# Seven tokens per row, earlier loads, and reciprocals on the GpSimd queue in an attention and maxout kernel

## The chip, the cores and the metric

The kernel runs on one core of one Trainium2 chip. The metric is the device time of one execution in microseconds (us). Before the change it was 395.11 us, the median of three runs (394.66 to 395.37).

The engines are called as in the profile: PE is TensorE, PEld its weight loads, ACT ScalarE, DVE VectorE, POOL GpSimd. SPq and POOLq are the DMA instructions that SyncE and GpSimd issue. Each engine works through its own list of instructions, and whatever stands at the head of the list holds what is behind it.

## The reference, cut to what matters

Softcapped attention feeds a maxout layer:

```python
# q, k, v: (8, 12, 448, 64) float32; w1, w2: (768, 1024); w_out: (1024, 768)
scores = 30 * tanh(scale * (q @ k.T) / 30)
attn = exp(scores - max) / sum(...)
x = (attn @ v) with heads side by side       # (3584, 768)
out = maximum(x @ w1, x @ w2) @ w_out         # (3584, 768) float32
```

## The kernel before

The 96 heads are worked in 48 pairs; one turn of the main loop, a "slot", is one pair. Three pairs form a group that is loaded and normalized together. The maximum is rewritten as x@w2 + relu(x@(w1-w2)), so the kernel first makes wd = w1-w2 and wm = w2@w_out (this is the "turn", "premultiply" and "subtract" below).

Three parts matter here. The first is how q and k arrive. A head has 448 rows, which is 3 x 128 + 64: partition p takes three neighbouring rows, and the last 64 rows come by transfers of their own. For the first four groups (12 pairs) TensorE turns them, and for the others a DMA transpose does:

```python
m, l = raw[g, what]                       # 3 x 128 rows, and the last 64
nc.sync.dma_start(out=m[...], in_=src[b, h0:h1, 0:NJ*P, :].rearrange("h (p j) d -> p h (j d)", j=NJ))
...                                       # [cut: one or two more for l]
for j in range(8):                        # transposes(i)
    nc.tensor.transpose(ps[:, j*P:(j+1)*P], kqf[g % 2][:, n, j, :], ident)
```

The second is the softmax sum. A row of sums leaves U, becomes 48 partitions, is inverted on VectorE, goes to DRAM and comes back broadcast to 64 partitions. All of these transfers are on the Sync queue. Then GpSimd multiplies:

```python
def invert(g, n0=0, n1=G):
    nc.vector.reciprocal(t[:m, :], sums[g, n0][:m, :])
    nc.sync.dma_start(out=d[:m, :], in_=t[:m, :])                  # rec_d <- rec_s
    for h in range(2):
        nc.sync.dma_start(out=rb[64*h:64*h+64, ...], in_=...to_broadcast(...))   # rec_b <- rec_d
def normalize(...):
    eng.tensor_mul(xT[b // 2][r, hp, cs], U[g][r, h, n, :], rec[g, n0][r, n - n0, :])
```

The third is the store of 128 finished rows. The row order of the output follows the row order of q:

```python
rows = out[b0*S : b0*S + NJ*P, :].rearrange("(p j) n -> p j n", j=NJ)
nc.sync.dma_start(out=rows[:, j, :], in_=osb)                      # 128 rows of 768
```

## Time and profile before

| | before |
|---|---|
| time, median of 3 runs | 395.11 us |
| span of the profiled run | 390.3 us |
| PE busy, PE idle | 358.5, 31.8 us |
| granted TensorE clock, mean | 0.983 |
| POOL busy | 199.6 us |

The busy lines and slices are shown in the prediction.

The waits of the kernel before: engine, line and tile that waited; what ended the wait; us in total, times, longest.

```profile
POOL xT L305 <- DMA rec_b<-rec_d: 73.8, 31, 8.3
DVE u L265 <- POOL xT L305: 24.7, 8, 4.5
```

GpSimd stands 73.8 us for broadcast reciprocals and this costs little, for TensorE waits for xT only 1.7 us. For the reciprocals GpSimd stands in this kernel only ahead of the multiplications that need the data.

### The profile page before, as it was taken

Reading aid. Unit: us, or ns where it says so; the run is one execution under the profiler, and the core shown is the slowest. Engines: PE = TensorE matmul, PEld = TensorE weight load, DVE = VectorE, ACT = ScalarE, POOL = GpSimd, SP = SyncE. Lnnn points to the kernel's source line nnn. Section 1 sums busy time; section 2 is a strip of 40 time slices with the busy share of each in tenths; the row PEclk is TensorE's granted clock in tenths of the full one; section 3 lists DMA queues with packets and bytes.
Section 4 is the critical chain, followed back from the end, with each engine's and each line's share of the span. In section 5 each row is a group of like instructions: output and inputs, shape, how many; then the busy total and the mean of one; then the engine's idle time right before and its main releaser. Section 6 shows DMA issues by size and latency. Waiting matters only on the chain.

```text
span 390.3 us, 5720 instructions
## 1 busy us (share of the span) xinstructions
PE 358.5 (92%) x2128; PEld 171.8 (44%) x2128; DVE 164.3 (42%) x248; ACT 292.4 (75%) x289; POOL 199.6 (51%) x254
## 2 busy tenths in 40 slices
PE   3468896999999999989998999999999999999995
PEld 1123443544444444434443445444444444455563
DVE  5332657774434533253325433352345333633421
ACT  2699995878899799978998899889998899400000
POOL 4272269674638374656657464729482733651000
PEclk9995998999999999999999999999999999999999
DMA  6998899786779768967989597969796751322022
GB/s 142 280 252 180 242 288 274 198 202 165 149 199 252 198 171 199 260 181 192 217 225 223 142 237 210 255 166 225 219 188 179 166 142 65 90 73 100 23 81 81
DMA packets 106596, 71.50 MB, mean 183 GB/s; under 512 B 61384, under 2 KB 99400, under 8 KB 106568
## 3 DMA queue, kind: packets, MB, share of 16 engines
q1 hardware_dynamic: 104616, 67.99, 67.6%
q0 software_dynamic: 1952, 3.15, 4.6%
q8 instruction: 16, 0.26, 0.3%
q14 instruction: 12, 0.10, 0.1%
HBM read 53.48 MB, written 11.18 MB: 166 GB/s over the span
## 4 chain that ended last, share of the span: by engine, by line
PE 54%; DMA 17%; ACT 7%; SPq 6%; POOL 6%; DVE 5%; issue 3%; POOLq 0%; DVEq 0%; ACTq 0%
PE mm L318 15%; PE mm L333 11%; PE mm L330 9%; PE pv L250 8%; DMA rec_d<-rec_s 7%; DMA rec_b<-rec_d 6%; POOL xT L305 6%; PE s L231 5%; ACT expo L238 3%; ACT tanh L232 3%; DMA vm<-in_v_dram 3%; PE pv L259 2%; SPq L112 2%; SPq L101 1%; DMA xT<-in_moe_w_dram 1%
## 5 line engine op out<-in xcount | busy, mean ns | idle before, releaser
L232 ACT ACTIVATE tanh<-s 128x896 bf16<-128x896 f32 x144 | 126.0, 909 | 36.2 <-PE s L231 35.9
L305 POOL TENSOR_TENSOR xT<-u,rec_b 64x448 bf16<-64x448 f32 x95 | 108.2, 1139 | 86.1 <-DMA rec_b<-rec_d 73.8
L238 ACT ACTIVATE expo<-tanh 128x1792 bf16<-128x1792 bf16 x96 | 144.9, 1510 | 3.0
L265 DVE COPY u<-pv 128x896 f32<-128x896 f32 x48 | 52.3, 1091 | 105.3 <-PE pv L259 80.6
L333 PE MATMUL mm<-wo_sb,gT 128*128 128x384 bf16 x448 | 88.8, 327 | 0.0
L318 PE MATMUL mm<-xT,wd_sb 128*128 128x448 bf16 x384 | 80.8, 353 | 3.3 <-POOL xT L305 1.7
L330 PE MATMUL mm<-wm_sb,xT 128*128 128x384 bf16 x336 | 68.0, 327 | 1.8 <-DVE osb L337 1.8
L250 PE MATMUL pv<-expo,vp 128*128 128x448 bf16 x288 | 66.3, 367 | 1.1 <-ACT expo L238 1.1
L333 PEld LDWEIGHTS <-gT 128*128 128x128 bf16 x448 | 41.9, 98 | 36.5 <-issue 10.8
L337 DVE COPY osb<-mm 128x384 f32<-128x384 f32 x56 | 31.0, 555 | 59.9 <-PE mm L333 54.9
L318 PEld LDWEIGHTS <-wd_sb 128*128 128x128 bf16 x384 | 35.4, 98 | 43.9 <-issue 14.5
L231 PE MATMUL s<-qkT 64*128 64x448 bf16 x288 | 46.0, 370 | 7.7 <-DVE qkT L210 5.2
L322 DVE TENSOR_SCALAR gT<-mm 128x448 bf16<-128x448 f32 x64 | 39.9, 623 | 29.6 <-PE mm L318 28.6
L330 PEld LDWEIGHTS <-xT 128*128 128x128 bf16 x336 | 31.7, 98 | 28.6 <-issue 8.7
L250 PEld LDWEIGHTS <-vp 128*128 128x128 bf16 x288 | 28.2, 101 | 29.1 <-issue 7.7
L132 POOL CAST kqf<-qm 128x1152 bf16<-128x1152 f32 x15 | 17.2, 1147 | 33.9 <-DMA qm<-in_q_dram 33.7
L235 ACT ACTIVATE tanh<-s 128x448 bf16<-128x448 f32 x48 | 26.0, 542 | 4.3 <-PE s L234 4.1
L124 POOL CAST vp<-vm 128x576 bf16<-128x576 f32 x30 | 19.9, 665 | 14.2 <-DMA vm<-in_v_dram 9.4
L132 POOL CAST kqf<-km 128x1152 bf16<-128x1152 f32 x15 | 17.2, 1147 | 12.7 <-DMA km<-in_k_dram 11.9
L231 PEld LDWEIGHTS <-qkT 64*128 64x128 bf16 x288 | 10.9, 96 | 22.8 <-issue 15.1
L209 PE MATMUL mm<-ident,kqf 128*128 128x128 bf16 x96 | 9.8, 248 | 11.5 <-DVE kqf L132 7.7
L186 PE MATMUL mm<-wo_sb,w2T 128*128 128x384 bf16 x96 | 18.7, 328 | 0.0
(44 smaller groups left out, 158.9 us busy)
## 6 DMA issues: line engine op xcount, KB each, us to landing
rec_b<-rec_d SPq DMA_DIRECT2D x30, 336.0 KB, 5.0
out_dram<-osb SPq DMA_DIRECT2D x24, 384.0 KB, 3.9
km<-in_k_dram SPq DMA_DIRECT2D x15, 576.0 KB, 7.0
qm<-in_q_dram SPq DMA_DIRECT2D x15, 576.0 KB, 4.5
vm<-in_v_dram SPq DMA_DIRECT2D x15, 576.0 KB, 4.4
xT<-in_moe_w_dram SPq DMA_DIRECT2D x6, 512.0 KB
wo_sb<-in_moe_w_out_dram POOLq DMA_DIRECT2D x4, 384.0 KB, 7.3
gT<-in_moe_w_dram POOLq DMA_DIRECT2D x6, 256.0 KB, 5.8
```

Of the source, the lines that this page charges most:

```text
L132: eng.tensor_copy(t[:, n0:n1, o : o + NJ, :].rearrange("p n j (h d) -> p n h j d", h=2), m[:, 2 * n0 : 2 * n1, :].rearrange("p (n h) (j d) ...
L231: nc.tensor.matmul(s[:, h, :S], t[r, j * P : (j + 1) * P], qTn[r, :])
L232: nc.scalar.activation(tanh[i][:, 2 * j : 2 * j + 2, :], s[:, :, :S], AF.Tanh, scale=scale / cap)
L238: nc.scalar.activation(expo[i][:, c0:c1, :], tanh[i][:, c0:c1, :], AF.Exp, scale=float(cap))
L250: nc.tensor.matmul(ps[:, h, :S], vp[g % 2][:, n, h, j, :], e[:, 2 * j + h, :], start=(j == 0), stop=False)
L265: nc.vector.tensor_copy(U[g][:, :, n, :], pvt[i][:, :, :S])
L305: eng.tensor_mul(xT[b // 2][r, hp, cs], U[g][r, h, n, :], rec[g, n0][r, n - n0, :])
L318: nc.tensor.matmul(ps[:, :S], wd_sb[:, c, f * P : (f + 1) * P], x[:, c, cs], start=(c == 0), stop=(c == KC - 1))
L322: nc.vector.tensor_relu(g[:, f, cs], ps[:, :S])
L330: nc.tensor.matmul(ps[:, : DM // 2], x[:, c, ts], wm_sb[:, c, hs], start=(c == 0), stop=False)
L333: nc.tensor.matmul(ps[:, : DM // 2], g[:, f, ts], wo_sb[:, f, hs], start=False, stop=(f == FC - 1))
L337: nc.vector.tensor_copy(osb[:, hs], ps[:, : DM // 2])
```

## The change

The intent is to take the start and one early hole away. In the first two batches, each partition takes seven neighbouring tokens (64 partitions a head, a run of 1,792 bytes), so k and q come in one transfer each. The price is 26 small transposes and one large one instead of eight, and another row order of the output. The reciprocals' transfers move from the Sync to the GpSimd queue, in two steps (invert, then spread), with casts placed around them. The w2 chunks still come one per slot, the first now ahead of the loop, and later groups are loaded earlier. In the loop, F(n) puts up to n matmuls of the weights' or the feed-forward part between the others.

```diff
+    def rows(t, b, h0, h1):
+        return t[b, h0:h1, :, :].rearrange("h (r j) d -> (h r) (j d)", j=R7)
...   [cut: loads and casts of k, q, v for the first four groups by these rows]
-        for j in range(8):
-            nc.tensor.transpose(ps[:, j * P : (j + 1) * P], kqf[g % 2][:, n, j, :], ident)
+        for c, to in todo:
+            for a in range(2):
+                r = slice(64 * a, 64 * a + 64)
+                nc.tensor.transpose(ps[r, to : to + 64], x[r, c : c + D], ident[r, r])
+        nc.tensor.transpose(ps[:, NJ * P : Q0], x[:, NJ * P : Q0], ident)
...
     def invert(g, n0=0, n1=G):
-        nc.sync.dma_start(out=d[:m, :], in_=t[:m, :])
+        nc.gpsimd.dma_start(out=d[:m, :], in_=t[:m, :])
+
+    def spread(g, n0=0, n1=G):
         for h in range(2):
-            nc.sync.dma_start(
+            nc.gpsimd.dma_start(
                 out=rb[64 * h : 64 * h + 64, : n1 - n0, :],
...
-                rows = out[b0 * S : b0 * S + NJ * P, :].rearrange("(p j) n -> p j n", j=NJ)
-                nc.sync.dma_start(out=rows[:, j, :], in_=osb)
+                if wide:
+                    ...   [cut: as before]
+                else:
+                    o = o.rearrange("(r j) n -> j r n", j=R7)
+                    nc.sync.dma_start(out=o[2 * j : 2 * j + 2, :, :], in_=osb)
...
-        e = 0 if g < NT else 2
+        e = 0 if g < NT else 2 if g < NT + 2 else 3
         at(3 * g - 6 - e, load, g, "k")
...   [cut: q, v and the casts follow; w2 chunk 1 + c in slot 1 + c; order of the start]
         F(4 if late else 8)
+        if i == N - 1:
+            invert(g, 0, G - 1)
+        elif i >= G and n == 0:
+            invert(g - 1)
...
         for f, a in todo[i]:
             f(*a)
+        if i == N - 1:
+            spread(g, 0, G - 1)
+        elif i >= G and n == 0:
+            spread(g - 1)
+        elif i >= G and n == 1:
+            normalize(g - 1)
...   [cut: the same calls taken away after the second F(6)]
```

More of the change, by code (lines that the diff above doesn't have):

```diff
@@ L40 @@
     NJ = 3
+    NT = 4
+    R7 = S // 64
     scale = 1.0 / (D ** 0.5)
@@ L69, with flat @@
     qf = [t[:, :, 4:8, :] for t in kqf]
+    def flat(g):
+        return kqf[g % 2].rearrange("p n j c -> p n (j c)")
     ident = const.tile([P, P], bf16, name="ident")
@@ L89, in half, with raw_of @@
         return slice(0, 64) if b % 2 == 0 else slice(64, P)
+    def rows(t, b, h0, h1):
+        return t[b, h0:h1, :, :].rearrange("h (r j) d -> (h r) (j d)", j=R7)
+    def raw_of(g, what):
+        if (g, what) not in raw:
+            raw[g, what] = stage.tile([P, 2 * L * NJ * D + (2 * L if what == "q" else L) * D], f32, name=what + "r")
+        t = raw[g, what]
+        m = t[:, : 2 * L * NJ * D].rearrange("p (h c) -> p h c", c=NJ * D)
+        l = t[:, 2 * L * NJ * D :].rearrange("p (h d) -> p h d", d=D)
+        return t, m, l
     def load(g, what, n0=0, n1=L):
@@ L94, in load @@
         src = {"k": k, "q": q, "v": v}[what]
-        if (g, what) not in raw:
-            raw[g, what] = (
-                stage.tile([P, 2 * L, NJ * D], f32, name=what + "m"),
-                stage.tile([P, 2 * L if what == "q" else L, D], f32, name=what + "l"),
+        t, m, l = raw_of(g, what)
+        if g < NT and what == "v":
+            x = rows(src, b, h0, h1).rearrange("(h r) c -> r h c", r=64)
+            for a in range(2):
+                nc.sync.dma_start(
+                    out=m[64 * a : 64 * a + 64, 2 * n0 : 2 * n1, :], in_=x[:, :, NJ * D * a : NJ * D * (a + 1)]
+                )
+            for par in range(2):
+                nc.sync.dma_start(
+                    out=l[64 * par : 64 * par + 64, n0:n1, :], in_=x[:, par::2, 2 * NJ * D :]
+                )
+            return
+        if g < NT:
+            nc.sync.dma_start(
+                out=t[:, n0 * S : n1 * S].rearrange("p (n c) -> p n c", c=S),
+                in_=rows(src, b, h0, h1).rearrange("(n p) c -> p n c", p=P),
             )
-        m, l = raw[g, what]
+            return
         nc.sync.dma_start(
@@ L119, in cast @@
         b = g * L // NP
-        m, l = raw[g, what]
+        x, m, l = raw_of(g, what)
         if what == "v":
@@ L128, in cast @@
                 eng.tensor_copy(vl[g % 2][r, n0:n1, r], l[r, n0:n1, :])
+            return
+        if g < NT:
+            x = x[:, n0 * S : n1 * S].rearrange("p (n c) -> p n c", c=S)
+            if what == "q":
+                eng.tensor_copy(flat(g)[:, n0:n1, Q0 : Q0 + S], x)
+                return
+            eng.tensor_copy(flat(g)[:, n0:n1, : NJ * P], x[:, :, : NJ * P])
+            for par in range(2):
+                r = slice(64 * par, 64 * par + 64)
+                eng.tensor_copy(kf[g % 2][r, n0:n1, 3, r], x[r, :, NJ * P :])
             return
@@ L207, in transposes @@
         ps = mm_psum.tile([P, 512], f32, name="mm").bitcast(bf16)
-        for j in range(8):
-            nc.tensor.transpose(ps[:, j * P : (j + 1) * P], kqf[g % 2][:, n, j, :], ident)
-        nc.vector.tensor_copy(qkT_of(g)[:, n, :, :].rearrange("p j c -> p (j c)"), ps)
+        x = flat(g)[:, n, :]
+        todo = [(j * D, (j % 3) * P + (j // 3) * 64) for j in range(6)]
+        odd = i // NP % 2
+        todo += [(Q0 + j * D, Q0 + (64 * j if not odd else 0 if j == 6 else 64 + 64 * j)) for j in range(R7)]
+        for c, to in todo:
+            for a in range(2):
+                r = slice(64 * a, 64 * a + 64)
+                nc.tensor.transpose(ps[r, to : to + 64], x[r, c : c + D], ident[r, r])
+        nc.tensor.transpose(ps[:, NJ * P : Q0], x[:, NJ * P : Q0], ident)
+        nc.vector.tensor_copy(qkT_of(g)[:, n, :, :].rearrange("p j c -> p (j c)")[:, : Q0 + S], ps[:, : Q0 + S])
     def cross(g):
@@ L221, in qk @@
         t = qkT[g][:, n, :, :].rearrange("p j c -> p (j c)")
-        o = Q0 + 64 * (i // NP % 2)
+        o = Q0 + (64 * (i // NP % 2) if g >= NT else 0)
         qTn = t[:, o : o + S]
@@ L278, in gather @@
             )
+    recd = {}
     def invert(g, n0=0, n1=G):
@@ L283, in invert @@
         nc.vector.reciprocal(t[:m, :], sums[g, n0][:m, :])
-        d = dram.tile([16 * G, 56], f32, name="rec_d")
-        nc.sync.dma_start(out=d[:m, :], in_=t[:m, :])
+        d = recd[g, n0] = dram.tile([16 * G, 56], f32, name="rec_d")
+        nc.gpsimd.dma_start(out=d[:m, :], in_=t[:m, :])
+    def spread(g, n0=0, n1=G):
         rb = rec[g, n0] = xpool.tile([P, G, S], f32, name="rec_b")
-        flat = d[:m, :].rearrange("(h n a) c -> h n (a c)", h=2, a=8)
+        lines = recd[g, n0][: 16 * (n1 - n0), :].rearrange("(h n a) c -> h n (a c)", h=2, a=8)
         for h in range(2):
-            nc.sync.dma_start(
+            nc.gpsimd.dma_start(
                 out=rb[64 * h : 64 * h + 64, : n1 - n0, :],
-                in_=flat[h : h + 1, :, :].to_broadcast([64, n1 - n0, S]),
+                in_=lines[h : h + 1, :, :].to_broadcast([64, n1 - n0, S]),
             )
@@ L337, in moe @@
                 nc.vector.tensor_copy(osb[:, hs], ps[:, : DM // 2])
+            wide = b * NP >= NT * L
             if t == 3:
                 for n in range(2):
-                    r0 = (b - 1 + n) * S + NJ * P
-                    nc.sync.dma_start(out=out[r0 : r0 + 64, :], in_=osb[64 * n : 64 * n + 64, :])
-            else:
-                b0, j = (b, t) if t < 3 else (b, t - 4)
-                rows = out[b0 * S : b0 * S + NJ * P, :].rearrange("(p j) n -> p j n", j=NJ)
-                nc.sync.dma_start(out=rows[:, j, :], in_=osb)
+                    o = out[(b - 1 + n) * S : (b + n) * S, :]
+                    to = o[NJ * P : S, :] if wide else o.rearrange("(r j) n -> r j n", j=R7)[:, R7 - 1, :]
+                    nc.sync.dma_start(out=to, in_=osb[64 * n : 64 * n + 64, :])
+            else:
+                j = t if t < 3 else t - 4
+                o = out[b * S : (b + 1) * S, :]
+                if wide:
+                    nc.sync.dma_start(out=o[: NJ * P, :].rearrange("(p j) n -> p j n", j=NJ)[:, j, :], in_=osb)
+                else:
+                    o = o.rearrange("(r j) n -> j r n", j=R7)
+                    nc.sync.dma_start(out=o[2 * j : 2 * j + 2, :, :], in_=osb)
     fill_q = []
@@ L358 @@
     NL = N // L
-    NT = 4
     todo = [[] for _ in range(N)]
@@ L365 @@
     for g in range(2, NL):
-        e = 0 if g < NT else 2
+        e = 0 if g < NT else 2 if g < NT + 2 else 3
         at(3 * g - 6 - e, load, g, "k")
-        at(3 * g - 5 - e, load, g, "q")
-        at(3 * g - 4, load, g, "v")
-        at(3 * g - (5 if e else 4), cast, nc.gpsimd, g, "k")
-        at(3 * g - (5 if e else 3), cast, nc.gpsimd, g, "q")
-        at(3 * g - 2, cast, nc.gpsimd, g, "v")
+        at(3 * g - 6 - max(e - 1, 0), load, g, "q")
+        at(3 * g - 4 - e, load, g, "v")
+        for what in "kq":
+            at(3 * g - (4 if g < NT else 5 if g < NT + 2 else 6), cast, nc.gpsimd, g, what)
         if g >= NT:
             at(3 * g - 4, cross, g)
-    at(1, cast, nc.gpsimd, 1, "v")
-    at(0, load_wo, 6)
     for c in range(KC):
-        at(1 + c, load_w2, c)
         at(2 + c, load_w1, c)
+    late_w2 = {1 + c: c for c in range(1, KC)}
     MS = 3
     fill_const(nc.vector, 0)
-    fill_const(nc.gpsimd, 1)
-    load_wo(0)
-    for n0, n1 in ((0, 1), (1, L)):
-        for what in "kqv":
-            load(0, what, n0, n1)
-    for what in "kqv":
-        load(1, what)
-    for what in "kq":
-        cast(nc.vector, 0, what, 0, 1)
+    load(0, "k", 0, 1)
+    load(0, "q", 0, 1)
+    load(0, "k", 1, L)
+    load(0, "q", 1, L)
+    load(0, "v", 0, 1)
+    load(1, "k")
+    load(0, "v", 1, L)
+    load(1, "q")
+    load(1, "v")
+    cast(nc.vector, 0, "k", 0, 1)
+    cast(nc.gpsimd, 0, "q", 0, 1)
+    fill_const(nc.gpsimd, 1)
     transposes(0)
-    cast(nc.vector, 0, "v", 0, 1)
-    for what in "kqv":
-        cast(nc.vector, 0, what, 1, L)
+    cast(nc.vector, 0, "k", 1, L)
+    cast(nc.vector, 0, "q", 1, L)
     qk(0, 0)
@@ L398 @@
     ex(0, 0, 4)
+    transposes(1)
     qk(0, 2)
@@ L401 @@
     ex(0, 4, 7)
+    cast(nc.vector, 0, "v")
     cast(nc.gpsimd, 1, "k")
-    load_wo(2)
     cast(nc.gpsimd, 1, "q")
-    load_wo(4)
-    transposes(1)
+    for f in range(0, FC, 2):
+        load_wo(f)
+    load_w2(0)
+    cast(nc.gpsimd, 1, "v")
     qk(1, 0)
@@ L438 @@
             ex(i + 1, 4, 7)
+        if i in late_w2:
+            load_w2(late_w2[i])
         for f, a in todo[i]:
             f(*a)
+        if i == N - 1:
[4 more added lines that the diff above has]
+            normalize(g - 1)
+        if i % L == 0 and 2 <= i // L + 1 < NL:
+            cast(nc.gpsimd, i // L + 1, "v")
         F(6)
@@ L444 @@
         F(6)
-        if i == N - 1:
-            invert(g, 0, G - 1)
-        elif i >= G and n == 0:
-            invert(g - 1)
-        if i >= G and n == 1:
-            normalize(g - 1)
         if i + 2 < N:
@@ L458 @@
     invert(N // G - 1, G - 1, G)
+    spread(N // G - 1, G - 1, G)
     normalize(N // G - 1, 0, G - 1)
```

## The prediction

> **What bounds the kernel now.** I read the page first (busy shares, the 40 slices), then the waits of the TensorE, then the timeline of the first 95 us and of the last 75 us. A "slot" below is one of the 48 head pairs, a "chunk" 128 rows of w1 or w2.
>
> The page of the kernel before:
> ```profile
> PE 358.5 (92%) x2128; PEld 171.8 (44%) x2128; DVE 164.3 (42%) x248; ACT 292.4 (75%) x289; POOL 199.6 (51%) x254
> ...
> PE   3468896999999999989998999999999999999995
> ...
> ACT  2699995878899799978998899889998899400000
> ...
> DMA  6998899786779768967989597969796751322022
> ```
> TensorE is busy for 358.5 of 390.3 us, so all its idle time is 31.8 us. The slices are 9.76 us wide: past the ninth TensorE reads 9 almost everywhere, while the DMA digits are 8 and 9 in the first seven. Summing busy time in stretches gives 67.4 us in the first 90 (22.6 idle), 246.6 from 90 to 340 (3.4 idle), 44.6 from 340 to the end (some 6 idle). So nothing is to be had in the long middle; a gain must come from the first 90 us. The waits of the TensorE name the causes:
> ```profile
> PE mm L209 <- DVE kqf L132: 7.7, 4, 4.1
> PE s L231 <- DVE qkT L210: 5.2, 5, 2.1
> PE mm L209 <- DVE wm_sb L191: 3.5, 3, 3.1
> ```
> The first two are the start: transposes waiting for k and q to be loaded and cast. The third is one hole of 3.1 us, at 62 us. ScalarE shows what both cost a pair (timeline, ScalarE):
> ```profile
> 17.14 1.73 ACT L232 ACTIVATE tanh<-s 128x896 bf16<-128x896 f32 x2 [2.96 <-PE s L231]
> ...
> 64.91 1.73 ACT L232 ACTIVATE tanh<-s 128x896 bf16<-128x896 f32 x2 [4.25 <-PE s L231]
> ```
> A pair needs 3 x 0.909 + 0.542 + 2 x 1.510 = 6.29 us of ScalarE (rows of the page). Pairs 0 to 3 have no other TensorE work beside them and go at that rate: first tanh at 8.13, 17.14, 23.40, 29.48, 35.56 us. Pair 0 to 1 took 9.0 instead of 6.3, and the step that ends at 64.91 took 10.6. The cause of the second, in the issues of the load queue and then VectorE:
> ```profile
> 41.16 0.35 SPq L285 DMA_DIRECT2D rec_d<-rec_s  x1
> 47.02 1.11 SPq L289 DMA_DIRECT2D rec_b<-rec_d  x2
> ...
> 52.95 0.59 SPq L165 DMA_DIRECT2D xT<-in_moe_w_dram  x1
> ```
> ```profile
> 58.73 2.10 DVE L168 TENSOR_TENSOR wd_sb<-xT,gT 128x1024 bf16<-128x1024 f32 x1 [2.97 <-DMA xT<-in_moe_w_dram]
> ```
> The queue stood from 41.2 to 47.0 for the reciprocals to come back from DRAM, then issued q and k, and only at 52.95 the third w1 chunk. VectorE, in order, waited for it until 58.73; behind it stood the copy of the pair's output (60.76) and the cast that TensorE waited for. Over the run that queue waits 56.3 us in all for reciprocals.
>
> **What the Trainium skill says.** "DMA: Bandwidth & Descriptors", Specifications: full rate needs 512 B or more. The page agrees that runs matter here: 61,384 of 106,596 packets are under 512 B, and the early DMA share is about 1.0 at 246 to 284 GB/s; no row shows the price of one size alone. The same table puts the first byte at about 1 us from the GpSimd queue against 0.6 from Sync; the trace shows medians to landing of 5.8 and 7.3 us for GpSimd loads and 5.0 for rec_b on Sync, of unlike sizes and loads. "TensorEngine Tiling (Array Packing)", Key Properties: a change of tiling mode drains the array; the trace agrees, some 0.1 us at each change between 128-row and 64-row matmuls (starts 0.28 apart where 0.19 would stream). Its Instruction Overhead (about 60 cycles however small the matmul) has no 64-column case in this trace.
>
> **The change part by part.**
> 1. *Rows of seven tokens, k and q of the first 12 pairs.* The main runs grow from 768 to 1,792 B (7 x 64 x 4), the 256-B remainders go, and k and q need one issue each instead of 3 and 2. Before, the first k, kl, kl, q issues stood at 0.75 to 3.15 us and q was cast at 5.38. Now q is issued second, near 1.3 us, and cast on GpSimd while VectorE casts k. I put the first tanh at 7.7 us (8.13 before; more transposes on a cold array eat much of the gain). k and q of pairs 1 and 2 follow at once instead of after eight issues, so they are no longer late: pair 1 starts at 7.7 + 6.3 = 14.0 instead of 17.14, say **-2.8 us**, as v may bite a little.
> 2. *Transposes.* 26 of 64x64 and one of 128x128 replace 8 of 128x128, for 12 pairs. Eight took 0.61 us warm, of which some 0.16 is the last one's pipeline: 0.055 each, 0.45 together. Two 64x64 ones can use different quadrants; if they go at about half the wide price the block is 27 x 0.027 = 0.75, serial at the wide price 1.5. With two mode changes of 0.1 the extra is 0.5 to 1.2 us a pair. In slots 0 to 2 it hides under ScalarE. In slots 3 to 9 TensorE has about 5.8 us of work (pair 2.7 with its transposes, w2 turn 0.45, premultiply 16 x 0.164 = 2.6) against ScalarE's 6.29, so a part hides again: seven slots at 0.35, **+2.5 us**.
> 3. *Reciprocals on the GpSimd queue.* The load queue no longer stands; the third w1 chunk can go at its planned slot, some 8 us earlier. The 10.6-us step becomes about 6.8: **-3.8 us**. GpSimd gains 49 issues; its own weight loads hold it 0.55 (L162) and 0.77 us (L157), so some 0.7 x 49 = 34 us on 199.6: it stays under 65% and is no bound.
> 4. *Middle.* Normalizing starts earlier in program order, but the hop is slower. Of 1.7 us waited for POOL xT and 1.1 for osb perhaps a third goes: **-0.8 us**.
> 5. *Tail.* Here the order turns against it: GpSimd must wait for the first reciprocals, issue two broadcasts, then do the same for the last pair, before it normalizes. VectorE had the last broadcast at 350.82:
> ```profile
> 350.82 0.62 DVE L305 TENSOR_TENSOR xT<-u,rec_b 64x448 bf16<-64x448 f32 x1 [4.46 <-DMA rec_b<-rec_d]
> ...
> 352.08 1.14 PE L330 MATMUL mm<-wm_sb,xT 128*128 128x384 bf16 x6 [1.77 <-DVE osb L337]
> ```
> TensorE already waits 1.77 us behind it. Four issues at 0.7 and two landings in series put it some 2 us later: **+2.0 us**.
> 6. *One w2 chunk per slot, casts moved.* Both kernels need chunk c at slot 3 + c; I count nothing.
>
> Sum: -2.8 + 2.5 - 3.8 - 0.8 + 2.0 = -2.9; 395.1 - 2.9 = **392 us**.
>
> **Rivals.** (a) *The transposes eat all of it*: if the small ones go one by one, part 2 is 9 slots x 1.0 = +9 us and the time is about 398. For it: TensorE is 87 to 89% busy there already. Against: the 64-row score matmuls do overlap in pairs (4 of 448 columns in 0.55 us). (b) *A new hole takes the place of the old*: w2 loads now stand on a GpSimd queue that also waits for reciprocals and normalizes for 7 us at a time, so a late chunk would stall the turn of w2 and with it TensorE; about 395. Against: each is issued a slot or more ahead. (c) *Loads no longer bind early*: slots 0 to 9 all run near ScalarE's 6.3 and the middle loses its 3.4 us of idle time; then -3 -4 -2 with part 2 nearly hidden and the tail unchanged, about 386.5. Against: more than 2% (7.9 us) is nearly all the idle time that I can name outside the first pair's unavoidable start.
>
> **Range and chances.** (c) gives the low end and (a) the high end of the range, a little inside. **392 us, 386.5 to 397.5.** Faster by over 2% means under 387.2, which needs (c) whole: 0.13. Slower by over 2% (over 403.0) needs (a) and (b) together: 0.03. Within 2%: 0.84.
>
> **What would show it.** Right: pair 1's first tanh near 14 us; no wait of wd_sb for w1 over 1 us and no 4-us gap of ScalarE near 60 us; twelve blocks of transposes 0.5 to 1.2 us longer; TensorE busy 362 to 368 us at a shorter span; the last VectorE multiplication about 2 us later against the last pair's end. Wrong: the waits of the transposes for kqf unchanged (loads not the cause of the start), waits of TensorE for GpSimd's casts or w2 in slots 3 to 9, POOL xT waits grown in the middle, or a tail that pays more than 4 us.

## More of the kernel before

The chain that ended last, as shares of the span by engine, has TensorE as more than half of it:

```profile
PE 54%; DMA 17%; ACT 7%; SPq 6%; POOL 6%; DVE 5%; issue 3%; POOLq 0%; DVEq 0%; ACTq 0%
```

## The result, and the profile after

The changed kernel took 419.76 us, the median of four runs (418.18 to 423.07), against 394.88 us for four runs of the kernel before. Ratios in this text are the mean time of one kernel's fast runs over that of the other's fast runs of the same rounds, so they are not quite the ratio of the quoted medians. Here the ratio is 1.065 (95% interval 1.057 to 1.073): slower by over 2%, and outside the predicted range. Both outputs agree with the reference.

The page of the changed kernel (busy time, then the 40 slices, now of 10.5 us, then the chain that ended last):

```profile
PE 369.5 (88%) x2356; PEld 175.2 (42%) x2356; DVE 159.8 (38%) x241; ACT 293.0 (70%) x289; POOL 225.7 (54%) x303
...
PE   3677969979995999888892999999989999978995
...
DMA  7999999492949779399799529796964451321021
...
DMA 32%; PE 28%; POOL 22%; issue 11%; ACT 3%; SPq 2%; DVE 2%; POOLq 0%; DVEq 0%
```

PE's idle time rose from 31.8 to 51.8 us and its busy time by 11.0 us, at a mean granted clock of 0.957 instead of 0.983: together the 31 us by which the span grew. The middle, which had nothing to give, has the holes: from 100 to 240 us PE stands 17.3 us (140 less 122.7 busy) against 2.4 before. In the chain TensorE fell from 54% to 28%, and POOL with DMA rose from 23% to 54%. DMA digits of 2 to 4 in the first half are new; before, none was under 6 there.

The waits of the TensorE in the changed kernel name other causes than before:

```profile
PE mm L371 <- POOL xT L358: 9.9, 5, 3.9
PE mm L257 <- DVE wm_sb L232: 5.7, 2, 3.8
...
PE mm L257 <- DVE kqf L166: 4.9, 2, 3.8
```

The last line is the start (7.7 us before). The first was 1.7 us. The second is the early hole, at 61.6 us, and it grew (3.5 us before). ScalarE's timeline answers to the two lines shown before:

```profile
13.95 1.73 ACT L281 ACTIVATE tanh<-s 128x896 bf16<-128x896 f32 x2
...
64.67 1.73 ACT L281 ACTIVATE tanh<-s 128x896 bf16<-128x896 f32 x2 [5.42 <-PE s L280]
```

Pair 1 starts at 13.95 instead of 17.14, as planned. The hole near 64 us did not close. The third w1 chunk was issued 9.4 us earlier (queue of the SyncE), but VectorE could not use it earlier by as much:

```profile
43.54 0.64 SPq L206 DMA_DIRECT2D xT<-in_moe_w_dram  x1
```
```profile
56.88 1.76 DVE L209 TENSOR_TENSOR wd_sb<-xT,gT 128x1024 bf16<-128x1024 f32 x1 [2.53 <-DMA xT<-in_moe_w_dram]
59.66 1.09 DVE L314 COPY u<-pv 128x896 f32<-128x896 f32 x1 [1.02 <-POOL xT L358]
...
379.79 0.66 DVE L358 TENSOR_TENSOR xT<-u,rec_b 64x448 bf16<-64x448 f32 x1 [7.08 <-DMA rec_b<-rec_d]
```

The second VectorE line says what ended last in the hole: the copy of the pair's output waits for a multiplication of GpSimd, and would have waited until about then for an earlier chunk too (the point on step 3 below shows it with e10 and e8). The third is the tail: 7.08 us for the last broadcast where it was 4.46. TensorE pays for that as well, and the timeline of the TensorE holds the small transposes too:

```profile
23.77 0.60 PE L257 MATMUL mm<-ident,kqf 64*64 64x64 bf16 x26
...
135.46 0.54 PE L371 MATMUL mm<-xT,wd_sb 128*128 128x448 bf16 x2 [3.18 <-DVE gT L375]
...
381.09 1.30 PE L383 MATMUL mm<-wm_sb,xT 128*128 128x384 bf16 x6 [4.42 <-DVE osb L390]
```

The stop of 3.18 us before 135.46 leads to a cause that I had not written down. Backwards from it: VectorE was late because it stood 3.50 us for the sums, to invert them at 134.44. Those sums had been issued at 121.87 (queue of the SyncE):

```profile
111.57 0.64 SPq L404 DMA_DIRECT2D out_dram<-osb  x1
...
118.47 3.03 SPq L404 DMA_DIRECT2D out_dram<-osb  x1
121.87 3.71 SPq L324 DMA_DIRECT2D sums<-u  x2
125.69 9.04 SPq L263 DMA_TRANSPOSE qkT<-kqf  x1
```

Ten kilobytes took 12.6 us (121.87 to 134.44), and the issue of a DMA transpose took 9.04 us where 12 of them had at most 4.83 before. Ahead of both in the queue are two stores of the new form. This is what the DMA engines did from 119 to 134 us, in 40 slices of 0.375 us (mean busy share of the 16 engines in tenths, and what they moved):

```profile
DMA  8966333111111111121217999111111111111117
GB/s 201 223 153 169 111 81 85 45 45 55 49 57 49 41 49 45 49 52 46 69 49 175 201 96 62 49 49 57 49 49 57 49 57 49 49 57 49 57 34 148
```

A steady digit of 1 at about 49 GB/s fits two of 16 engines (a share of 0.125; the mean share is 0.14 from 122 to 126 us and 0.13 from 129 to 133.4). A store of 384 KB (393 kB) at 49 GB/s is 8.0 us by estimate, two are 16 us, and from the issue of the second to the end of the plateau, at about 133.6, there are 15 us, as if most of the first was still to be moved. The view doesn't name the transfers; that they are the stores is shown by e10 and e13 below. The same stretch of the loop before moves 246 GB/s on average against 78 (kernel before, the same view, 115 to 130 us):

```profile
DMA  7799999999999817559999999999999766499999
```

The Trainium skill had said so. "DMA: Bandwidth & Descriptors", section "Why a DMA increments its semaphore by 16 and not by 1", under "How many engines (k)", says that a transfer uses the largest k up to 16 that divides the slowest dimension over 1 of both access patterns. Its section "Rules for kernel authors", row "Use all 16 engines", warns that an outermost dimension of c < 16 confines the transfer to c engines. The new store's DRAM side is [2, 64, 768]: two. The trace agrees (share 0.13 to 0.14; 49 GB/s over two engines is 24.5 each). I had read the page for run lengths and passed over this.

The other part of the chain is GpSimd. Its waits, and VectorE's for it, in the changed kernel:

```profile
POOL rec_d L336 <- DVE rec_s L334: 51.0, 12, 8.2
POOL xT L358 <- DMA rec_b<-rec_d: 45.7, 24, 4.9
POOL rec_b L342 <- DMA rec_d<-rec_s: 36.0, 13, 7.0
DVE u L314 <- POOL xT L358: 29.7, 7, 11.0
```

The waits in the first and third lines stand ahead of two DMA issues. What is behind them on GpSimd (casts, w2 loads, multiplications) stands as well. I had counted the issues and not these 87 us.

### The profile page after: what moved, and what is told of

Its sections match the earlier page's. It is cut to its first block, busy times and chain, and to the rows that moved or that the text cites. A ratio compares the mean times of both kernels' runs of the same rounds, so it can differ in the third digit from the quotient of the medians.

```text
span 421.3 us, 6105 instructions
## 1 busy us (share of the span) xinstructions
PE 369.5 (88%) x2356; PEld 175.2 (42%) x2356; DVE 159.8 (38%) x241; ACT 293.0 (70%) x289; POOL 225.7 (54%) x303
## 4 chain that ended last, share of the span: by engine, by line
DMA 32%; PE 28%; POOL 22%; issue 11%; ACT 3%; SPq 2%; DVE 2%; POOLq 0%; DVEq 0%
DMA rec_b<-rec_d 19%; POOL xT L358 16%; DMA rec_d<-rec_s 8%; PE mm L386 7%; PE mm L371 7%; PE mm L383 5%; PE pv L299 4%; DMA vr<-in_v_dram 4%; POOL kqf L173 3%; PE s L280 2%; ACT expo L287 1%; ACT tanh L281 1%; POOL rec_b L342 1%; PE pv L308 1%; SPq L263 1%
## 5 line engine op out<-in xcount | busy, mean ns | idle before, releaser
L371 PE MATMUL mm<-xT,wd_sb 128*128 128x448 bf16 x384 | 87.2, 372 | 16.5 <-POOL xT L358 9.9
L386 PE MATMUL mm<-wo_sb,gT 128*128 128x384 bf16 x448 | 90.2, 331 | 0.0
L371 PEld LDWEIGHTS <-wd_sb 128*128 128x128 bf16 x384 | 36.6, 101 | 61.7 <-issue 34.4
L336 POOL DMA_DIRECT2D rec_d<-rec_s x17 | 9.4, 554 | 55.1 <-DVE rec_s L334 51.0
L342 POOL DMA_DIRECT2D rec_b<-rec_d x34 | 17.8, 527 | 36.1 <-DMA rec_d<-rec_s 36.0
L154 POOL CAST vp<-vr 128x576 bf16<-128x576 f32 x30 | 20.1, 669 | 0.4
L257 PE MATMUL mm<-ident,kqf 64*64 64x64 bf16 x312 | 8.8, 209 | 12.1 <-DVE wm_sb L232 5.7
```

Source lines behind the costliest of these rows:

```text
L371: nc.tensor.matmul(ps[:, :S], wd_sb[:, c, f * P : (f + 1) * P], x[:, c, cs], start=(c == 0), stop=(c == KC - 1))
L386: nc.tensor.matmul(ps[:, : DM // 2], g[:, f, ts], wo_sb[:, f, hs], start=False, stop=(f == FC - 1))
```

## The experiments

After the result there were these theories. **Standing**: GpSimd holds its other work while it waits to issue the reciprocals. **Stores**: the two-engine stores hold the Sync queue. **Loads**: the earlier loads and casts crowd the first half. **Buffer**: two U buffers tie VectorE to a later GpSimd. **Rows**: the small transposes cost too much. In e1 to e9 the stores were not yet a theory of mine, so those expectations argue about the others.

The outputs of all agree with the reference within its tolerance. One of them, e13, is wrong (row order): in the reference's output the rows of one batch differ from their mean by 1% of the output's size (4.7e-5 against 4.6e-3, root mean square), so that the comparison cannot see their order. That the changed kernel's rows are in order rests on its code alone. "Before" in a row is the kernel before, run on the same chip in the same rounds (seven runs each).

| run | median us | before us | ratio (95% interval) |
|---|---|---|---|
| e1_rec_sync | 411.51 | 393.97 | 1.047 (1.041 to 1.054) |
| e2_before_rec_pool | 425.52 | 393.97 | 1.081 (1.075 to 1.087) |
| e3_rec_undone | 432.85 | 393.97 | 1.097 (1.086 to 1.109) |
| e4_old_loads | 418.35 | 393.97 | 1.064 (1.058 to 1.070) |
| e6_rows_old_loads_rec_undone | 420.94 | 395.20 | 1.067 (1.057 to 1.076) |
| e7_before_new_loads | 397.42 | 395.20 | 1.006 (1.000 to 1.012) |
| e8_after_u3 | 415.65 | 395.20 | 1.051 (1.044 to 1.059) |
| e9_before_u3 | 392.33 | 395.20 | 0.992 (0.987 to 0.998) |
| e10_split_stores | 401.09 | 393.43 | 1.020 (1.014 to 1.027) |
| e11_rows_split | 390.15 | 393.43 | 0.993 (0.986 to 1.000) |
| e12_rec_sync_split | 386.24 | 393.43 | 0.986 (0.976 to 0.996) |
| e13_before_two_row_stores | 423.21 | 393.43 | 1.074 (1.063 to 1.085) |
| e14_rec_d_sync | 398.97 | 394.27 | 1.013 (1.006 to 1.020) |
| e15_rec_b_sync | 390.05 | 394.27 | 0.981 (0.974 to 0.988) |
| e16_tail_sync | 395.39 | 394.27 | 1.002 (0.998 to 1.007) |

Four runs of each; all are fast except one of e3, one of e13 and two of e15, which the ratios leave out (and one run of the kernel before in e1 to e4 and e10 to e13). The medians are of all runs. A program on one core counts as slow when it is over 1.5% above its fastest run.

### e1_rec_sync: the reciprocals back on the Sync queue, at their new places

```diff
 (after; invert and spread)
-        nc.gpsimd.dma_start(out=d[:m, :], in_=t[:m, :])
+        nc.sync.dma_start(out=d[:m, :], in_=t[:m, :])
-            nc.gpsimd.dma_start(
+            nc.sync.dma_start(
                 out=rb[64 * h : 64 * h + 64, ...
```

> The changed kernel with the reciprocals' three transfers back on the Sync queue, at the same places in the program. Theory Q (the GpSimd queue is the cause: its sequence stands in order for the reciprocal, for rec_d and for rec_b, 133 us in all, so normalizing is late and VectorE and TensorE wait behind it): 388 to 396 us, GpSimd's wait for rec_s and rec_d gone. Rival L (earlier loads and casts fill the DMA queue, so that sums and reciprocals land late): still 410 or more. Rival P (the reciprocal earlier in VectorE's order): still about 410.

It took 411.51 us: about 8 us came back, and 17.5 us of loss stayed. So the queue alone was not the whole of it, and something else in the change is slow.

### e2_before_rec_pool: only the queue change, on the kernel before

```diff
 (before; invert)
-        nc.sync.dma_start(out=d[:m, :], in_=t[:m, :])
+        nc.gpsimd.dma_start(out=d[:m, :], in_=t[:m, :])
-            nc.sync.dma_start(
+            nc.gpsimd.dma_start(
```

> The kernel before with only the reciprocals' transfers moved to the GpSimd queue, at their old place. Theory Q: 410 or more, as the queue alone suffices. Rival L: 394 to 400, since the loads and casts are the old ones. Rival P: 394 to 400.

It took 425.52 us, 8% more than before. Here rec_d and its broadcasts are issued back to back, and everything on GpSimd stands for both (waits of this run):

```profile
POOL rec_b L289 <- DMA rec_d<-rec_s: 59.6, 17, 6.0
POOL rec_d L285 <- DVE rec_s L283: 55.9, 14, 6.8
...
DVE u L265 <- POOL xT L305: 55.8, 11, 9.0
```

There are no new stores, loads or rows here, so the standing is a cause by itself. VectorE's wait for GpSimd's multiplications is 55.8 us where it was 24.7, and TensorE's is 11.4 where it was 1.7.

### e3_rec_undone: e1 with the calls at their old places too

```diff
 (e1)
-        elif i >= G and n == 0: invert(g - 1)         # after F(8)
...
-            spread(g - 1)                              # after the slot's loads and casts
-        elif i >= G and n == 1: normalize(g - 1)
...
         F(6)
+        elif i >= G and n == 0: invert(g - 1); spread(g - 1)
+        if i >= G and n == 1: normalize(g - 1)
```

> The changed kernel with the reciprocals on the Sync queue and reciprocal, broadcast and normalizing at their old places; rows of seven tokens, the new transposes and the earlier loads and casts stay. Theory Q: 388 to 395. Rival L: 410 or more. Rival P: 388 to 395, and then e1 is slow.

It took 432.85 us: taking back all that concerns the reciprocals made it slower than the change itself. With the queue as it was (e1), the new places are worth 21 us here. The Sync queue held the hops up: one rec_d was issued at 204.48 us, behind a two-row store, and its broadcasts only at 214.78. Such gaps led to the stores later.

### e4_old_loads: the loads and casts of the later groups at their old slots

```diff
 (after)
-        e = 0 if g < NT else 2 if g < NT + 2 else 3
+        e = 0 if g < NT else 2
...
-        at(3 * g - 4 - e, load, g, "v")
+        at(3 * g - 4, load, g, "v")
...   [cut: casts at their old slots]
```

> The changed kernel with the loads and casts of groups 4 and up at their old places; reciprocals stay on the GpSimd queue. Theory Q: still 410 or more. Rival L: 388 to 398. Rival P: still 410 or more.

It took 418.35 us, within the spread of the changed kernel (418.18 to 423.07). The earlier loads are not the cause in the changed kernel.

### e6_rows_old_loads_rec_undone: only rows, small transposes, start and w2

The edits of e3 and of e4 together.

> Only the first two batches' part of the change (rows of seven tokens, small transposes, new order of the start, w2 chunks spread); loads of groups 4 and up, reciprocals, broadcasts and normalizing as before. Theory of two harms (the reciprocals on GpSimd in e2, and the earlier loads in front of the reciprocals on one Sync queue in e3, each make normalizing late): 388 to 394 us. Rival R (the rows or the small transposes carry the harm of e1 and e3): 410 or more.

It took 420.94 us, 6.7% over before, with neither the reciprocals nor the loads changed. Something in what was left costs as much as the whole change. PE stood idle for 53.4 us (419.7 - 366.3) against 31.8 before, and its 7.8 us more of busy time came at a granted clock of 0.957 instead of 0.983, so more work is not shown. What was left includes the stores, because the rows bring them.

### e7_before_new_loads: only the earlier loads, on the kernel before

```diff
 (before)
-        e = 0 if g < NT else 2
+        e = 0 if g < NT else 2 if g < NT + 2 else 3
...
-        at(3 * g - 4, load, g, "v")
+        at(3 * g - 4 - (e if e > 2 else 0), load, g, "v")
...   [cut: the casts follow by one slot]
```

> The kernel before with only the loads and casts of groups 4 and up moved earlier as in the change. Theory of two harms: 405 to 430 us, with long waits of GpSimd for rec_b and of VectorE's u copy for normalizing. Rival R: 392 to 398.

It took 397.42 us, a ratio of 1.006. Earlier loads alone are harmless. (The edit leaves v of groups 4 and 5 at its old slots, which the change moves too.) (Beside slow stores and Sync-queue hops they are not: e3 has them and e6 has not, by ratios 1.097 and 1.067.)

### e8_after_u3 and e9_before_u3: a third U buffer

```diff
 (after for e8, before for e9)
-    upool = ctx.enter_context(tc.tile_pool(name="upool", bufs=2))
+    upool = ctx.enter_context(tc.tile_pool(name="upool", bufs=3))
-        t = xpool.tile([16 * G, 56], f32, name="rec_s")
+        t = xpool.tile([16 * G, 56], f32, name="rec_s", bufs=1)
```

The second edit only makes room.

> The changed kernel with a third buffer for the pairs' outputs (and one buffer less for a small reciprocal tile, to fit). Loop theory (late normalizing hurts because VectorE's copy of a pair's output waits for its buffer to be normalized, and everything behind it on VectorE waits too): 388 to 400 us, the wait of u for POOL xT near 0. Rival X (the direct wait of the feed-forward matmuls for normalized rows is what costs): 412 or more, that wait grown.

> The kernel before with the same third buffer, the control of e8. Loop theory: the loop does not bind here, 391 to 395 us. Rival X: the same.

They took 415.65 and 392.33 us. VectorE's wait for a free U buffer is gone from e8's waits, and yet TensorE waits as much as ever for the multiplications (10.6 us against 9.9). So the buffer is worth about 4 us beside these delays and 0.8% without them. It is not the way by which most of the loss comes.

### e10_split_stores: each two-row store as two one-row stores

```diff
 (after)
-                    nc.sync.dma_start(out=o[2 * j : 2 * j + 2, :, :], in_=osb)
+                    for a in range(2):
+                        nc.sync.dma_start(out=o[2 * j + a, :, :], in_=osb[64 * a : 64 * a + 64, :])
```

The bytes, rows and place are the same; the outermost dimension is now 64, which by the rule quoted above lets 16 engines share it.

> The changed kernel with each of the six stores of 2 x 64 rows of the first two batches cut into two stores of 64 rows; all else as changed. Theory S (a store whose DRAM side has an outermost dimension of 2 runs on 2 of the 16 DMA engines, holds them for some 10 us each, and every small transfer of sums and reciprocals behind it waits): the DMA share in the 10 us after each store no longer falls to 0.1, and the time falls to 388 to 404 us. Rival Q (the reciprocals on the GpSimd queue): still 410 or more.

It took 401.09 us, a ratio of 1.020 instead of 1.065: the stores cost some 18 us of the changed kernel (0.045 x 394 us by ratios, 18.7 us by medians). The plateau is gone (DMA view of e10, 113 to 128 us, 40 slices):

```profile
DMA  5999999986999989997997999831010002999999
```

A stretch of some 2.6 us with almost no DMA is left, from about 122.8 us; its cause was not followed. TensorE in the middle is whole again: from 100 to 240 us it stands 2.6 us (140 less 137.4), where the changed kernel had 17.3.

### e11_rows_split and e12_rec_sync_split: the same edit on e6 and on e1

> e6 (rows of seven tokens and small transposes alone) with the same split stores. Theory S: 386 to 394 us, since only the start and the transposes of the change are left. Rival T (the small transposes or the seven-token loads do harm later): 410 or more.

> e1 (the change with the reciprocals on the Sync queue) with the same split stores. Theory S: 386 to 394 us; the difference to e10 is what the GpSimd queue costs in the changed kernel, which I put at 0 to 12 us. Rival: 405 or more as in e1.

They took 390.15 and 386.24 us. The kernel e6 went from 1.067 to 0.993 by the split alone, and e1 from 1.047 to 0.986. So the rest of e6's loss was the stores. The version with everything of the change except the reciprocals' queue and the two-row stores, e12, is faster than the kernel before, by 1.4% (0.4 to 2.4). Its page has PE at 93% and no digit under 9 after the ninth slice but the last:

```profile
PE 357.5 (93%) x2356; PEld 172.2 (45%) x2356; DVE 160.4 (42%) x241; ACT 292.2 (76%) x289; POOL 199.5 (52%) x252
...
PE   2786988979999999999999999999999999999995
```

PE busy is 357.5 us where it was 358.5, although 228 more matmul records are there; the granted clock was higher too (0.993 instead of 0.983), so this shows that the small transposes cost little, not that they cost nothing. The e10 and e12 kernels differ in nothing but the reciprocals' queue, and by 401.09 - 386.24 = 14.9 us (13.5 by ratios).

TensorE's idle time says where each of the two losses lies (us, in three stretches of each profiled run):

| | 0 to 100 | 100 to 320 | 320 to the end |
|---|---|---|---|
| before | 22.6 | 2.8 | 6.3 |
| e12 | 21.0 | 0.0 | 5.7 |
| e10, with the queue | 26.0 | 2.8 | 8.6 |
| the change, with the stores too | 24.1 | 18.4 | 9.3 |

The queue costs 5.0 us of idle time ahead of 100 us and under 3 in each of the other stretches; the rest of its loss is busy time at a lower clock (361.3 us at 0.983 in e10, 357.5 at 0.993 in e12). The stores cost in the middle.

### e13_before_two_row_stores: the new stores alone, on the kernel before (wrong row order on purpose)

```diff
 (before; b < 2 only)
+            elif b < 2:
+                j = t if t < 3 else t - 4
+                o = out[b * S : (b + 1) * S, :].rearrange("(r j) n -> j r n", j=7)
+                nc.sync.dma_start(out=o[2 * j : 2 * j + 2, :, :], in_=osb)
```

The rows of the first two batches land in the wrong order, since the kernel before does not hold them by sevens; the 64-row stores of these batches go to the seventh row likewise. Nothing else differs.

> The kernel before with only the stores of the first two batches written as in the change, two outer rows of 64 (its rows then lie in the wrong order: the result is wrong on purpose, bytes and sizes are the same). Theory S: 410 to 425 us, all the loss between 105 and 250 us. Rivals Q and T: 393 to 397.

It took 423.21 us, 7.4% more. The queue of the SyncE, first a new store, then a rec_d and its broadcasts:

```profile
106.83 0.64 SPq L346 DMA_DIRECT2D out_dram<-osb  x1
107.57 0.99 SPq L285 DMA_DIRECT2D rec_d<-rec_s  x1
118.06 1.16 SPq L289 DMA_DIRECT2D rec_b<-rec_d  x2
```

The queue could not issue the broadcasts for 10.5 us after the rec_d (10.5 KB), where the kernel before took 4.1 (108.47 to 112.55). Only the form of the store ahead of it is new, and the DMA view shows the plateau again, some 50 GB/s from about 110 to 116.6 us. So the two-row stores are a cause by themselves, the second one beside standing.

### e14_rec_d_sync and e15_rec_b_sync: one half of the reciprocals' way each on the Sync queue, stores split

```diff
 (e10)
 e14:  invert:  nc.gpsimd.dma_start(out=d...)   ->  nc.sync.dma_start(out=d...)
 e15:  spread:  nc.gpsimd.dma_start(out=rb...)  ->  nc.sync.dma_start(out=rb...)
```

What remained open was which of GpSimd's two stands costs the 15 us: the one before rec_d, the one before the broadcasts, or the longer tail.

> e10 with only the transfer of the reciprocals to DRAM (rec_d) on the Sync queue; the broadcasts stay on GpSimd. If GpSimd's standing for the reciprocal (46 us of waits in e10) is what delays its casts and multiplications: 387 to 391 us, near e12. If the standing for rec_d ahead of the broadcasts is the cause: 397 to 402, as e10.

> e10 with only the broadcasts (rec_b) on the Sync queue; rec_d stays on GpSimd. If the standing for rec_d ahead of the broadcasts (28 us of waits in e10) is the cause: 387 to 391 us. If the standing for the reciprocal is: 396 to 402.

With rec_d on Sync it took 398.97 us (1.013 against 1.020 of e10): little. With the broadcasts on Sync it took 390.05 us in the median of all four runs; its two fast runs were 384.42 and 388.19, a ratio of 0.981. That is as good as e12; it rests on two runs, but all four (390.05 against 394.27) are far from e10's 1.020 too. Slower landing from the GpSimd queue is not the reason: the broadcasts land in 5.7 us from issue in e10 and in e15 alike (medians of the pages). GpSimd's timelines show what differs. In e10 the casts stand behind the broadcasts' issue:

```profile
86.97 0.55 POOL L336 DMA_DIRECT2D rec_d<-rec_s  x1 [1.82 <-DVE rec_s L334]
92.69 1.05 POOL L342 DMA_DIRECT2D rec_b<-rec_d  x2 [5.17 <-DMA rec_d<-rec_s]
...
99.28 4.70 POOL L358 TENSOR_TENSOR xT<-u,rec_b 64x448 bf16<-64x448 f32 x4
```

In e15 the same casts fill the time in which rec_d lands and comes back:

```profile
83.32 0.56 POOL L336 DMA_DIRECT2D rec_d<-rec_s  x1 [1.82 <-DVE rec_s L334]
...
88.94 0.50 POOL L178 CAST kqf<-qr 64x384 bf16<-64x384 f32 x1
92.78 1.13 POOL L358 TENSOR_TENSOR xT<-u,rec_b 64x448 bf16<-64x448 f32 x1 [3.33 <-DMA rec_b<-rec_d]
```

From the issue of rec_d to the first multiplication it is 12.3 us in e10 and 9.5 us in e15, and in e10 5.5 us of casts (93.8 to 99.3) follow the stand instead of lying inside it. Over the run e15 still stands 56.9 us for rec_s, which is more than e10's 46.2, and it costs no more for that. In e14 the one remaining stand grew from 27.7 to 70.7 us. So the wait for rec_d's landing ahead of the broadcasts is the one that costs. (The tail is in this too, for e15 moves its broadcasts with the others.)

### e16_tail_sync: the last group's reciprocals alone on the Sync queue, stores split

```diff
 (e10; rec_d and rec_b)
-        nc.gpsimd.dma_start(
+        (nc.sync if g == N // G - 1 else nc.gpsimd).dma_start(
```

> e10 with the transfers of the last group alone on the Sync queue. From the traces of e10 and e12 the tail is worth about 3 of the 15 us (TensorE waits 4.1 us for osb there against 0.9): 397 to 399 us. If the tail is most of it: under 392.

It took 395.39 us, 5.7 us under e10's median (1.002 against 1.020). It was run at another time. The traces give the tail its size: from the start of ScalarE's last exp to the end it is 58.5 us in e10 (340.08 to 398.6), 54.3 in e16 (340.11 to 394.4) and 54.4 in e12. So the tail is 4.2 us of what the queue costs, more than the prediction's 2.0, and some 10 us lie ahead of it: e12 begins that exp at 329.78.

## Why the prediction was right or wrong, point by point

The prediction of 392 us was wrong by 28 us, in the direction to which it gave 3%.

- **Omitted step, the stores: +18 us.** "The change part by part" claims to list what the change adds, and its six parts do not contain the stores, though the diff does. No rival had them either. Alone they cost 30 us (e13), within the change 18 to 19 (e10).
- **Step 3, the reciprocals on the GpSimd queue: the step that failed.** It said "some 0.7 x 49 = 34 us on 199.6: it stays under 65% and is no bound". Both numbers were about right: there were 51 issues, not 49, and POOL rose by 26.1 to 225.7 us, 54%. The conclusion did not follow. At 54% GpSimd was on the path, because it stood ahead of work that others need, and the standing (51.0 + 36.0 us) was not priced. Where steps 3 to 5 together expected a gain (-3.8 - 0.8 + 2.0 = -2.6 us), the queue alone costs 14.9 (e10 against e12). Moving the broadcasts alone back brings it all back (e15); 4.2 us of it lie in the tail (e16) and some 10 ahead of it. One of the prediction's own signs of being wrong came with it: TensorE's waits for POOL xT grew in the middle, from 1.7 to 9.9 us.
- **Step 3, the w1 chunk.** The issue moved as predicted (52.95 to 43.54), but the subtraction began at 56.88 instead of 58.73 and still stood 2.53 us. The step of ScalarE that was to shrink to 6.8 us took 11.5 (53.20 to 64.67). Before it was 10.3 (54.61 to 64.91); the prediction's 10.6 is a slip. What ended last was not the chunk but GpSimd's multiplications (59.66 above). In e10 the subtraction (56.03) waits for nothing, and the copy behind it still stands 3.40 us for them; with a third U buffer (e8) the copy stands for nothing and the step is 8.0 us. In e12 the chunk goes at 43.17, as early as in the change though the hops are on Sync, and the step is 8.2 us (52.30 to 60.47): 2.1 us gained against 3.8 predicted. So the hole could be closed in part, and not by this queue.
- **Step 1, the start: right, the 14.0 in part by luck.** First tanh at 6.81 us (predicted 7.7), pair 1 at 13.95 (predicted 14.0): the first came 0.9 us early, and the step took 7.1 us instead of 6.3, for ScalarE stood 0.95 us for TensorE at 11.21. TensorE then waited 2.48 us for v at 15.65, and pair 2 began at 21.72 instead of 23.40: of the 3.2 us gained at pair 1, 1.7 were left. The step had said that "v may bite a little". Whether the longer runs or the fewer issues and their new order brought the gain was not separated; the packet counts of the page, which the prediction read as agreeing, show no rate.
- **Step 2, the transposes: mis-sized.** Predicted 0.5 to 1.2 us more a pair and +2.5 us in all. In the trace 26 small ones take 0.60 us (0.53 to the next start, at 24.30, so 20 ns each where 27 were assumed) and the block 0.76 us, against 0.61 for the eight before: +0.15 us, for twelve pairs some 1.8 us of TensorE by estimate, mode changes not counted. How much of it is on the path was not measured alone, but e11, which has them all, is no slower than the kernel before (0.993). Rival (a) falls with it.
- **Step 5, the tail.** The direction was right, and VectorE's last wait grew by 7.08 - 4.46 = 2.6 us against 2.0. But from the start of ScalarE's last exp to the end the change takes 59.7 us (361.63 to 421.3) where 55.0 were taken before (335.31 to 390.3): 4.7 us, of which moving the hops gives back 4.2 (e16). The term was short by more than half, and more than 4 us was the prediction's own sign of being wrong.
- **Rival (b)**, a new hole in place of the old, had the right engine ("a GpSimd queue that also waits for reciprocals and normalizes"), but only w2 was followed behind it, and it was put at +3 us. The w2 loads were not what was late; the multiplications and casts were.
- **Rival (c)**, about 386.5, is near what e12 reached (386.24), as a change that keeps the hops on Sync and splits the stores. It needed both of the parts that went wrong to be left out. The match of the numbers is in part luck: e12's rounds had the kernel before at 393.43, and its ratio of 0.986 on the prediction's 395.1 is 389.6. The middle did lose its idle time, as (c) says (0.0 us from 100 to 320), but the step near 60 us stayed at 8.2 us.

The account, by medians: 393.4 before, -7 for the rows, start, places and earlier loads (e12), +15 for the queue (e10), +19 for the stores (the change). By ratios it is -1.4%, +3.4% and +4.5%. The signs of the first test, on the kernel before, are the same but the sizes are not additive: +32 for the queue alone (e2), +30 for the stores alone (e13), +25 for the whole change with both. Each delays the same multiplications, and the new places of the calls may soften the queue's part, which no run tests. How much of each lies in the shadow of the other was not separated, and stays open. Neither was why earlier loads are harmless alone (e7) and cost some 12 us beside slow stores and Sync-queue hops (e3 against e6).

Of the versions here e12 and e15 beat both kernels, by 1.4% and 1.9% against the kernel before. Their intervals overlap, so which of the two is better is not decided, nor is whether either is over 2%.

## What to carry to other kernels

When a layout changes, follow it to the store, and for each transfer read the outermost dimension of both access patterns: six stores of [2, 64, 768] cost 18.7 us here, where the rest of the change without its queue won 7.2, and cutting each in two by the outer dimension took it back. Before moving a chain of dependent transfers to another engine's queue, price what stands behind each wait, not the issues: put the waiting half on a queue with less urgent work behind it (Sync here, by e15), or place the useful work between the two halves (in the change itself, with one group's casts placed so, the stand ahead of the broadcasts at 114.88 us was 0.75 us). GpSimd's busy share of 54% told neither.

## What the Trainium skill lacked or had wrong

- "DMA: Bandwidth & Descriptors", the rules on the number of engines, was right and I overlooked it: a share of 0.13 to 0.14, about 49 GB/s. What it lacks is the price for what is queued behind: 10 KB of sums took 12.6 us, a DMA transpose's issue 9.04 us instead of at most 4.83, and the whole kernel 7.4% (e13).
- The same page, section "Rules for kernel authors", row on spreading DMAs over SP, ACT and GpSimd, says that it only saves the sequencer's issue time. The runs show that the choice of the issuer also decides what stands while a dependent transfer waits: 14.9 us between e10 and e12, 8% between e2 and the kernel before. The page does say, in its section "Anatomy of one DMA", that a semaphore wait happens on the issuing sequencer before dispatch (here 51.0 + 36.0 us of GpSimd's time), but neither it nor another page puts that beside the choice of the issuer or gives a cost.
- "TensorE: Matmul & The Clock Gate", section "Wait — 56ns, not 53.3ns?", gives a floor of about 25 ns from start to start however small a matmul is. Here 26 transposes of 64x64, in turn on two quadrants of the array, went at 20 ns each (0.53 us from the first to the start of the next group, warm). The page does not say whether its floor holds across quadrants.
